# Column-tiled lone score tiles, the sync queue in the scheduler, and newly searched limits in an attention kernel

## The chip, the cores and the metric

The kernel runs on one core of one Trainium2 chip. The metric is device time in microseconds (us). A ratio is the mean time of one kernel's fast runs over that of the kernel before in the same rounds, so it is not quite the ratio of the medians that stand beside it.

In the profile lines, PE is the matrix engine TensorE, PEld its weight load, DVE is VectorE, ACT is ScalarE, POOL is GpSimd, and SP is the sync engine that issues most transfers ("SPq").

## The reference, cut to what matters

Two attention layers read the same input, and a gate mixes their results. Layer A is full softmax attention with 32 heads of size 16 over 2048 positions. Layer B is a local one with a window of 8.

```python
def _A_ref(x, wqkv, wo):
    ...                                   # q, k, v = x @ wqkv, H = 32 heads, Dh = 16
    scores = jnp.einsum("bhqd,bhkd->bhqk", q, k) * Dh ** -0.5
    o = jnp.einsum("bhqk,bhkd->bhqd", softmax(scores), v)
    return o... @ wo
def _B_ref(x, wqkv, wo): ...              # keys at distance 0, 2, .., 14 only
g = sigmoid((x * gate_w).sum(-1, keepdims=True))
return g * _A_ref(x, A_wqkv, A_wo) + (1 - g) * _B_ref(x, B_wqkv, B_wo)
```

## The kernel before

The scores of A are cut into 2048 tiles of 128 keys by 512 queries. They are worked through in 32 blocks of 64 tiles (one query chunk and one set of four heads per block). Each tile's exponential is computed either by ScalarE (`pt`), two or three tiles at a time, or by VectorE (`yb`), which approximates it with integer arithmetic: one pass per tile and two more passes over batches of up to four tiles. Only six of the sixteen key tiles (`KD`) may go to VectorE. A score matmul reads 32 rows (four heads' 16-wide keys sit in four row groups), so it is row-tiled; nearly every other matmul of the kernel is column-tiled (128 rows, 32 columns, four at a time).

The instruction order is not written by hand. While the kernel is built, a list scheduler in Python plays a timeline with its own constants (a matmul counts 0.216 us, a switch of tiling mode 0.11 us) and emits each instruction when its turn comes. Its decisions depend on limits such as these; eleven of them are given per stretch, 64 stretches in all, as strings of digits.

```python
MM = 0.216
SWITCH = 0.11
D_LAST = 58
...
def d_wanted(now, flex=True):            # may a tile go to VectorE now?
    if p >= N - 8 or p % 64 >= D_LAST or not any(k in KD for r in rem[p // 64] for k in r):
        return False                     # p: number of score tiles handed out so far
    ...
    ready = [s for s in self.steps if s.rel <= p and s.eng in ("PE", "DVE") and ready_time(s) <= now + 1.5]
    ...
    load = max(0.0, t["DVE"] - now) + sum(s.cost for s in ready if s.eng == "DVE")
    return load < tune("backlog" if flex else "backlog_s")
...
# TensorE has nothing better to do: a "lone" tile for VectorE, by itself
elif fits(MM + SWITCH - tune("alone")) and d_wanted(now) and self.kq_ok(rem, geo, p, 4, now):
    emit_qk([d_take([])], [], now)
...
# transfers: s.n is the number of issues, T_SP = 0.55 us each
sp = now0 + s.n * T_SP
```

The sixteen small copies of the gate are issued inside a VectorE step (`gate_t`), so this account of the queue doesn't see them.

## Time and profile before

| | before |
|---|---|
| time, median (of three runs) | 733.99 us (732.43 to 734.55) |
| span in the profile | 731.1 us |
| busy ACT, DVE, PE | 705.8, 673.8, 694.4 us |
| score tiles exponentiated by DVE, by ACT | 526, 1522 |

From the page of the kernel before: busy times, then the span in 40 slices, each digit the busy share in tenths.

```profile
span 731.1 us, 20619 instructions
...
PE 694.4 (95%) x8304; PEld 225.8 (31%) x8304; DVE 673.8 (92%) x1149; ACT 705.8 (97%) x704; POOL 206.5 (28%) x218
...
DVE  6897999998999999999999999999999998998884
ACT  6998999999999999999999999999999999999994
```

ScalarE is the limit: it is full from the third slice to the last but one, save for the fourth, where the stall shown below lies. VectorE has some room all along, so the way to be faster is to move tiles from ScalarE to VectorE. The groups of instructions by shape (count | busy us, mean ns of one | idle time before them and what ended it) show what a tile costs:

```profile
L1855 ACT ACTIVATE pt<-fps 128x1024 bf16<-128x1024 f32 x546 | 531.0, 1089 | 8.4 <-PE fps L1801 6.4 <-PE fps L1605 1.2
L1533 DVE TENSOR_SCALAR yb<-fps 128x512 int16<-128x512 f32 x526 | 340.4, 683 | 21.5 <-PE fps L1801 20.0
...
L1855 ACT ACTIVATE pt<-fps 128x1536 bf16<-128x1536 f32 x143 | 217.4, 1520 | 2.9 <-PE fps L1801 2.4
```

ACT handles 546 x 2 + 143 x 3 tiles in these, and one more by itself, in 700 us: 0.46 us a tile. VectorE waited 20 us in all for a score matmul (line 1801) to give it a tile.

The timeline of TensorE around a lone tile (start, duration, instruction, count). Durations of matmuls include their latency; what counts is the distance of the starts.

```profile
401.69 0.39 PE L1605 MATMUL fps<-pt,vaug 128*32 128x512 bf16 x1
401.69 0.40 PE L1605 MATMUL fps<-yb,vaug 128*32 128x512 f16 x2
401.70 0.39 PE L1605 MATMUL fps<-pt,vaug 128*32 128x512 bf16 x1
402.02 0.38 PE L1801 MATMUL fps<-qm,kT 32*128 32x512 bf16 x1
402.33 0.40 PE L1517 MATMUL fps<-wz 128*32 128x512 bf16 x4
```

The row-tiled tile starts 0.32 us after the four column-tiled matmuls and holds the next ones off for 0.31 us; where four column-tiled matmuls follow four others, the starts are about 0.22 us apart (405.30 and 405.52 us in the same trace).

One stall stands out. The waits of TensorE, the sync queue's issues between 30 and 64 us, and the table of windows (busy us of each engine in each stretch, then granted clock, DMA share, GB/s):

```profile
PE fps L881 <- DMA ww<-in_B_wqkv_dram: 2.7, 1, 2.7
```

```profile
36.80 10.78 SPq L1121 DMA_DIRECT2D gA<-gs  x16
47.69 10.64 SPq L948 DMA_DIRECT2D qm<-qs  x16
58.37 0.58 SPq L876 DMA_DIRECT2D ww<-in_B_wqkv_dram  x1
```

```profile
54.00:58.00 4.00, 4.00 (x59) 1.42 (x59) 3.97 (x8) 4.00 (x5) 1.30 (x2) 1.00 0.11 27
58.00:62.00 4.00, 1.34 (x22) 0.43 (x21) 1.06 (x3) 1.59 (x3) 4.00 (x5) 1.00 0.18 41
62.00:66.00 4.00, 4.00 (x39) 0.76 (x30) 2.70 (x4) 3.37 (x3) 0.77 (x1) 0.57 0.00 0
```

The columns after the stretch's length are PE, PEld, DVE, ACT, POOL. A weight load is issued only at 58.4 us, behind 32 small copies that took the queue 21 us, and all of TensorE, VectorE and ScalarE stand still for it.

### The profile page before, as it was taken

What the parts mean: (1) busy time and instruction counts of PE and PEld (TensorE: products, weight loads), DVE (VectorE), ACT (ScalarE), POOL (GpSimd) and SP (SyncE); (2) the same over time, 40 slices, a digit from 0 to 9 for tenths busy, and PEclk for the clock granted to TensorE, in tenths of its full rate; (3) what the DMA queues carried; (4) which work ended last, traced back from release to release, by engine and by line L of the source; (5) the groups of instructions that cost most, each with busy time, mean ns of one, the idle gap of its engine ahead of it and who ended that gap; (6) DMA issues with size and microseconds to landing.
All of it is one profiled execution on the core that took longest, in us unless ns stands there. A gap on an engine that the chain in (4) does not pass through costs nothing.

```text
span 731.1 us, 20619 instructions
## 1 busy us (share of the span) xinstructions
PE 694.4 (95%) x8304; PEld 225.8 (31%) x8304; DVE 673.8 (92%) x1149; ACT 705.8 (97%) x704; POOL 206.5 (28%) x218
## 2 busy tenths in 40 slices
PE   9998999999998999999999999999999999999996
PEld 4432333333332323332222323323222322222342
DVE  6897999998999999999999999999999998998884
ACT  6998999999999999999999999999999999999994
POOL 2134000000003322222000456555545635256100
PEclk9999999999999999999999999999999999999999
DMA  6000201000000100001033446474464552284000
GB/s 167 3 13 22 58 2 39 1 30 4 8 8 1 24 1 6 4 1 39 8 71 101 120 112 163 127 174 125 127 162 114 155 147 79 75 181 116 9 31 28
DMA packets 63720, 48.54 MB, mean 66 GB/s; under 512 B 21760, under 2 KB 63232, under 8 KB 63488
## 3 DMA queue, kind: packets, MB, share of 16 engines
q1 hardware_dynamic: 62912, 45.70, 24.8%
q8 instruction: 67, 1.10, 0.6%
q0 software_dynamic: 288, 1.05, 0.4%
q14 instruction: 37, 0.30, 0.2%
q10 hardware_dynamic: 416, 0.39, 0.2%
HBM read 39.85 MB, written 5.26 MB: 62 GB/s over the span
## 4 chain that ended last, share of the span: by engine, by line
ACT 39%; PE 30%; DVE 13%; issue 11%; SPq 2%; DMA 2%; POOL 1%; ACTq 0%; DVEq 0%; POOLq 0%
ACT pt L1855 38%; PE fps L1801 11%; PE fps L1605 10%; PE fps L881 7%; DVE yb L1533 6%; DVE yb L1539 3%; SPq L948 2%; DMA vw<-v_dram 1%; PE fps L1350 1%; DVE prod L1201 1%; POOL erb L1332 1%; DVE t L1637 1%; PE fps L1215 1%; PE fps L954 0%; ACT er L1220 0%
## 5 line engine op out<-in xcount | busy, mean ns | idle before, releaser
L1855 ACT ACTIVATE pt<-fps 128x1024 bf16<-128x1024 f32 (+1 forms) x690 | 700.0, 1178 | 11.4 <-PE fps L1801 8.8
L1533 DVE TENSOR_SCALAR yb<-fps 128x512 int16<-128x512 f32 x526 | 340.4, 683 | 21.5 <-PE fps L1801 20.0
L1801 PE MATMUL fps<-qm,kT 32*128 32x512 bf16 x2048 | 308.8, 383 | 21.5 <-ACT pt L1855 16.0
L1605 PE MATMUL fps<-pt,vaug 128*32 128x512 bf16 (+1 forms) x1618 | 247.9, 374 | 0.1
L1801 PEld LDWEIGHTS <-kT 32*128 32x128 bf16 x2048 | 91.0, 91 | 283.3 <-issue 276.1
L1539 DVE TENSOR_SCALAR yb<-yb 128x2048 int16<-128x2048 int16 (+3 forms) x280 | 177.7, 665 | 0.8
L1605 PE MATMUL fps<-yb,vaugw 128*32 128x512 f16 (+1 forms) x1116 | 163.8, 372 | 2.1 <-DVE yb L1539 2.0
L881 PE MATMUL fps<-xT,ww 128*32 128x512 bf16 (+2 forms) x1296 | 99.4, 381 | 4.4 <-DMA ww<-in_B_wqkv_dram 2.7
L1332 POOL TENSOR_TENSOR er<-er,vw 128x512 bf16<-128x512 bf16 x64 | 72.4, 1156 | 108.3 <-DMA erb<-er_dram 63.7
L1605 PE MATMUL fps<-yb,vaug 128*32 128x512 f16 (+1 forms) x558 | 99.3, 372 | 0.1
L1605 PEld LDWEIGHTS <-vaug 128*32 128x32 bf16 x2176 | 68.2, 94 | 95.2 <-issue 87.8
L1332 POOL TENSOR_TENSOR erb<-erb,vw 128x512 bf16<-128x512 bf16 x64 | 73.2, 1164 | 72.8 <-DVE yb L1539 28.8
L1201 POOL TENSOR_TENSOR prod<-bq,bk 128x512 bf16<-128x512 bf16 x32 | 34.0, 1075 | 128.1 <-DVE yb L1539 78.9
L1605 PEld LDWEIGHTS <-vaugw 128*32 128x32 bf16 x1116 | 44.2, 95 | 41.6 <-issue 35.9
L881 PEld LDWEIGHTS <-ww 128*32 128x32 bf16 x1296 | 26.4, 95 | 36.3 <-issue 25.1
L1201 DVE TENSOR_TENSOR prod<-bq,bk 128x2048 bf16<-128x2048 bf16 x24 | 28.7, 1222 | 0.4 <-PE fps L1215 0.4
L1628 DVE STREAM_TRANSPOSE t<-fps 128x512 f32<-128x512 f32 x32 | 22.7, 709 | 4.5 <-PE fps L1605 4.5
L1124 POOL DMA_DIRECT2D wAv<-in_A_wo_dram x1 | 0.8, 757 | 85.4 <-PE fps L1801 85.4
L881 PE MATMUL fps<-woB,oB 128*32 128x512 bf16 x256 | 20.5, 383 | 0.0
L881 PE MATMUL fps<-wAv,oT 128*32 128x512 bf16 x256 | 19.5, 384 | 0.1
L881 PE MATMUL fps<-wAv,xT 128*32 128x128 bf16 (+1 forms) x512 | 18.3, 274 | 0.0
L909 DVE CAST vaug<-fps 128x384 bf16<-128x384 f32 (+1 forms) x24 | 12.2, 509 | 4.8 <-PE fps L881 4.4
(112 smaller groups left out, 277.7 us busy)
## 6 DMA issues: line engine op xcount, KB each, us to landing
vw<-v_dram SPq DMA_DIRECT2D x128, 128.0 KB, 3.2
er<-er_dram SPq DMA_DIRECT2D x128, 64.0 KB, 3.0
erb<-er_dram SPq DMA_DIRECT2D x128, 64.0 KB, 2.9
v_dram<-vs SPq DMA_DIRECT2D x16, 128.0 KB, 3.0
out_dram<-ob SPq DMA_DIRECT2D x15, 128.0 KB, 1.7
qm<-qs SPq DMA_DIRECT2D x112, 16.0 KB, 1.8
x_in<-in_A_x_dram SPq DMA_DIRECT2D x3, 512.0 KB, 6.1
ww<-in_B_wqkv_dram SPq DMA_DIRECT2D x12, 128.0 KB, 2.7
```

What stands on the lines that cost most here:

```text
L881: self.nc.tensor.matmul(out=out_ps[32 * c:32 * c + 32, 0:n], lhsT=lhsT_of(c), rhs=rhs, start=start, stop=stop, tile_position=(0, 32 * c))
L909: self.nc.vector.tensor_copy(out=self.vaug4[:, st0:st0 + nst, h0:h1, 0:DH], in_=self.misc[:, 0:nst * n].rearrange("p (t h e) -> p t h e", ...
L948: self.nc.sync.dma_start(out=self.qm[i % NQM][r][k:k + 16, :], in_=self.qs[i % 2][k:k + 16, :])
L1201: return e.tensor_tensor(out=pr[m % 2][:, a:b], in0=bq[ct][:, a:b], in1=bk[ct][:, o + a:o + b], op=ALU.mult)
L1215: nc.tensor.matmul(out=self.misc[32 * sc:32 * sc + 32, :], lhsT=self.Eh[:, ct, :], rhs=pr[m % 2][:, sc * 512:(sc + 1) * 512], start=(ct == ...
L1332: return nc.gpsimd.tensor_tensor(out=st_["erb"][m % 4][:, g, :], in0=st_["erb"][m % 4][:, g, :], in1=st_["vw"][m % 2][:, g, :], op=ALU.mult)
L1533: return nc.vector.tensor_scalar(out=self.yb[bt["buf"]][:, 0, i * 512:(i + 1) * 512], in0=bank[:], scalar1=A, scalar2=1024.0 * (15.0 + PW_ ...
L1539: return nc.vector.tensor_scalar(out=y[:, k, 0:n], in0=y[:, 0, 0:n], scalar1=float(round(1024.0 * (PW_S[k] - PW_S[0]))), scalar2=None, op0 ...
L1605: nc.tensor.matmul(out=out, lhsT=v, rhs=r, start=start, stop=stop, tile_position=(0, 32 * j))
L1628: nc.vector.transpose(out=self.t1[:, par].rearrange("p a b -> p (a b)"), in_=self.flex[acc[b]])
L1801: nc.tensor.matmul(out=dst, lhsT=self.kT[ct % 2][32 * j:32 * j + 32, kt * 128:(kt + 1) * 128], rhs=self.qm[(4 * ct + qc) % NQM][par][32 * ...
L1855: nc.scalar.activation(out=self.pt[pi[0]][pi[1]][:, 0:n * 512], in_=self.aslot[si][:, 0:n, :].rearrange("p a b -> p (a b)"), func=ACT.Exp, ...
```

## The change

Its intent, in three parts. (1) Lone tiles need no change of tiling mode: for key tile 9, each head's keys are copied into a tile of 128 rows that is zero elsewhere, so that a score matmul can use all 128 rows and be split into four column tiles. (2) The scheduler's account of the sync queue includes the gate copies, and some issue counts are raised. (3) All limits and several constants are set anew; a beam search chose the digits of the 64 stretches.

```diff
+KZ = (9,)
+TUNE = dict(R0=74, R1w=42, R1g=20, ..., ahead=0.142, ..., dlast=62, ..., prelB=59, prodrel=-12)
 LEVELS = dict(                      # every level list replaced
-    backlog=(1.5, 2.2, 3.0, 3.8, 5.0),
+    backlog=(0.758, 1.231, 1.61, 1.894, 2.273, 2.841, 3.788),
 ...
 STRETCH = dict(                     # every string replaced
-    grab="2222222222222222222222222222222222122221222222222222222222212222",
+    grab="0000040200000000000000000000000000000200040020000000000000000030",
 ...
+        self.kz = c([P, 4, len(KZ), P], BF16, name="kz")           # zeroed once
-        self.wz = c([P, 512], BF16, name="wz")                      # makes room for kz
+        self.wz = c([P, P], BF16, name="wz")
+    def k_spread(self, ct, kt):
+        for j in range(4):
+            r = slice(32 * j, 32 * j + 32)
+            self.nc.sync.dma_start(out=self.kz[r, j, KZ.index(kt), :], in_=self.kT[ct % 2][r, P * kt:P * kt + P])
...
-                wl = self.dma(... self.load_w("B", kind, ct), 6.0, rel=R0 + 16 * n - 44)
+                wl = self.dma(... self.load_w("B", kind, ct), 6.0, rel=R0 + 16 * n - U["prelB"])
-        self.gate_done = Step("DVE", 1.5, gate_t, deps=[ch[-1]], due=50, cls=1, lat=4.0)
+        self.gate_done = Step("DVE", 1.5, gate_t, deps=[ch[-1]], due=50, cls=1, lat=14.0)
+        self.gate_done.dn = 19                                       # issues in the sync queue
...
-        R0 = 64                                                      # branch B's projections start from this score tile on
+        R0 = U["R0"]                                                 # 74
...
-            if p >= N - 8 or p % 64 >= D_LAST or ...
+            if p >= N - 8 or p % 64 >= TUNE["dlast"] or ...
-            ready = [... ready_time(s) <= now + 1.5]
+            ready = [... ready_time(s) <= now + TUNE["ahead"]]
...
+        def emit_alone(d, now):
+            for c in range(4):
+                nc.tensor.matmul(out=dst[32 * c:32 * c + 32, :], lhsT=self.kz[:, j, KZ.index(kt), 32 * c:32 * c + 32],
+                                 rhs=self.qm[(4 * ct + qc) % NQM][par][:], start=True, stop=True, tile_position=(0, 32 * c))
+            t["PE"] = now + k * MM + (SWITCH if mode == "r" else 0.0)
+            mode = "c"
...
-                    elif fits(MM + SWITCH - tune("alone")) and d_wanted(now) and self.kq_ok(...):
+                    elif spread(now) and fits(MM - tune("alone")) and d_wanted(now):
+                        emit_alone(d_take([], True), now)
+                    elif not spread(now) and fits(MM + SWITCH - tune("alone")) and d_wanted(now) and self.kq_ok(...):
```

More of the change, by code (lines that the diff above doesn't have):

```diff
@@ L53 @@
 YB_ITEMS = 4
+TUNE = dict(R0=74, R1w=42, R1g=20, R2g=31, R3g=46, R3w=50, dueB=61, dueL=84, v2rel=79, v2step=21, v2due=91, krel=230, krel2=192, ahead=0.142, dueV=30, dueS=115, dueO=678, dlast=62, qrel=28, prelB=59, prodrel=-12)
 LEVELS = dict(
-    backlog=(1.5, 2.2, 3.0, 3.8, 5.0),
-    backlog_s=(0.5, 1.0, 1.5, 2.2, 3.0),
-    part_us=(1.5, 2.2, 3.0, 4.0, 6.0),
-    misc_slack=(-20, -8, 0, 8, 20),
-    urgent=(0, 4, 8, 16, 32),
-    fit=(-0.2, 0.0, 0.2, 0.4, 0.6),
-    port=(0.3, 0.6, 0.9, 1.2, 2.0),
@@ L63 @@
-    alone=(-9.0, -0.2, 0.0, 0.2, 9.0),
-    grab=(0, 1, 4, 2, 1),
-    lend=(0, 1, 3, 2, 7),
-    order=((-1, 1, 0, 2, 3), (-1, 0, 2, 1, 3), (-1, 0, 1, 2, 3), (-1, 0, 1, 2, 1), (1, 0, 1, 2, 3)),
+    backlog=(0.758, 1.231, 1.61, 1.894, 2.273, 2.841, 3.788),
+    backlog_s=(0.888, 1.442, 1.886, 2.219, 2.663, 3.329, 4.438),
+    part_us=(0.6, 0.975, 1.275, 1.5, 1.8, 2.25, 3.0),
+    misc_slack=(-32, -18, -12, -8, -4, 2, 16),
+    urgent=(-25, -11, -5, -1, 3, 9, 23),
+    fit=(0.0, 0.2, 0.3, 0.4, 0.5, 0.6, 0.8),
@@ L67 @@
+    port=(0.338, 0.549, 0.718, 0.845, 1.014, 1.268, 1.69),
+    alone=(-8.973, -0.273, -0.123, 0.027, 0.177, 0.327, 9.027),
+    grab=(1, 0, 2, 3, 4),
+    lend=(1, 0, 2, 3, 4, 5, 6, 7),
+    order=((-1, 0, 1, 2, 1), (-1, 1, 0, 2, 3), (-1, 0, 2, 1, 3), (-1, 0, 1, 2, 3), (1, 0, 1, 2, 3), (0, 0, 1, 2, 3), (1, 0, 2, 1, 3), (2, 0, 1, 2, 3)),
 )
 STRETCH = dict(
-    backlog="1111111111131111111111111111111111111111111111111111211111111111",
-    backlog_s="3333333333333333333333333333333333333333333333333333133333333233",
@@ L71 @@
-    part_us="0000010000040000000000000000000000000000000000000000000000000000",
-    misc_slack="1111111111111111111111111111111111111111111111111111111111111111",
-    urgent="0000000000000000000000000000000000000000000000000000000000000000",
-    fit="3333333333333333333333333333333333333333333333333333333333333332",
-    port="2222222222232222222222222222222222222222222222222222432222222222",
-    alone="2222221222122222222222222222222222322222222222222222122212222222",
-    grab="2222222222222222222222222222222222122221222222222222222222212222",
@@ L78 @@
-    lend="1111111111111111111111111111111111011111111111111111111111111111",
-    order="4144444444444444444444444444444444444144444444444444444444444444",
+    backlog="3333333333333333333633333333433363534333333336633333333333334336",
+    backlog_s="3333333333333333333333330333333323353333333333333433333332333033",
+    part_us="3353333536333603130313333336033313303333443333303332433333333333",
+    misc_slack="3333331333333333333333333333235533333333033233333333333333333333",
+    urgent="3333333433333333333333333333364313333336233333333333335333333333",
@@ L80 @@
+    fit="3533331313633333333333333303333332333303133533333333133303333333",
+    port="3333333333333333333333333333433334333333334433333333543333633333",
+    alone="3331332033330333333333333333335323333333333333333333433333333333",
+    grab="0000040200000000000000000000000000000200040020000000000000000030",
+    lend="0000000300060000000001000000500000000000000000002000600000000000",
+    order="1000000700000000000005410000407010000000400000000000100200000000",
 )
 SLOT_D = 3
-D_LAST = 58
 X_LAND = (0, 1.7, 3.7, 5.2)
@@ L702 @@
     __slots__ = ("eng", "cost", "fn", "deps", "due", "cls", "rel", "acq", "free", "lat", "end", "on_done", "hold",
-                 "chain", "port", "n")
+                 "chain", "port", "n", "dn")
     def __init__(self, eng, cost, fn, deps=(), due=0.0, cls=2, rel=-1, acq=False, free=False, lat=0.1,
@@ L711, in __init__ @@
         self.n = 1
+        self.dn = 0.0
 T_ACT = lambda n: n / 1200.0 + 0.063
@@ L833, in setup @@
         nc.vector.memset(warm[:], 0.0)
-        nc.vector.memset(self.wz[:, P:512], 0.0)
         nc.scalar.activation(out=warm[:], in_=warm[:], func=ACT.Exp)
@@ L851, in setup @@
         nc.gpsimd.memset(self.vaug[:, NKT * H * VS:NKT * H * VS + 32], 0.0)
+        nc.gpsimd.memset(self.kz[:], 0.0)
         for w, v, v4 in zip(PW_W[1:], self.vw[1:], self.vw4[1:]):
@@ L1040, in jobs @@
                 wl = self.dma(lambda ct=ct: (self.load_w("A", "k", ct), self.load_w("A", "q", ct)), 6.0,
-                              rel=base - 290)
+                              rel=base - 290, n=2)
             for sc in range(4):
@@ L1053, in jobs @@
                     if ct:
-                        rel = base - 230 + 16 * sc
+                        rel = base - TUNE["krel"] + 16 * sc
                         if ct >= 2:
-                            rel = base - 64 * 3 + 16 * sc
+                            rel = base - TUNE["krel2"] + 16 * sc
                     else:
@@ L1066, in jobs @@
                         ("DVE", T_D1(512), lambda ct=ct, sc=sc: self.q_stage(ct, sc))],
-                        due=qd - 8, rel=base + 128 * sc - 128 * (NQM - 1) + 4, deps=dep)
+                        due=qd - 8, rel=base + 128 * sc - 128 * (NQM - 1) + TUNE["qrel"], deps=dep)
                     qd = [ch[-1]]
@@ L1075, in jobs @@
                     qdone[(ct, sc)] = self.dma(lambda ct=ct, sc=sc: self.q_split(ct, sc), T_LAND, deps=qd,
-                                               n=16 if (ct, sc) == (3, 3) else 8)
+                                               n=20 if (ct, sc) == (3, 3) else 10)
         for st in range(0, NKT, 2):
@@ L1088, in jobs @@
                                  for k in range(1, NP_) if st in KD],
-                            due=512 - 100 + 4 * st, rel=80 + 20 * st)
+                            due=512 - TUNE["v2due"] + 4 * st, rel=TUNE["v2rel"] + TUNE["v2step"] * st)
             for ct in range(1, 4):
@@ L1092, in jobs @@
         self.kdone, self.qdone, self.vdone = kdone, qdone, vdone
+        self.kzdone = {(ct, kt): self.dma(lambda ct=ct, kt=kt: self.k_spread(ct, kt), T_LAND, deps=[kdone[(ct, kt // 4)]],
+                                          rel=512 * ct if ct else 4, due=512 * ct + 16 * (kt // 4), n=4)
+                       for ct in range(4) for kt in KZ}
         self.xs = xs
@@ L1143, in b1_open @@
                 pr[i] = BP["1"].tile([P, S], BF16, name=f"prod{i}")
-        R0 = 64
+        U = TUNE
+        R0 = U["R0"]
         o1 = self.dma(b1_open, 0.5, rel=R0, deps=self.x_done)
@@ L1171, in jobs_b @@
             for kind in ("q", "k"):
-                wl = self.dma(lambda ct=ct, kind=kind: self.load_w("B", kind, ct), 6.0, rel=R0 + 16 * n - 44)
+                wl = self.dma(lambda ct=ct, kind=kind: self.load_w("B", kind, ct), 6.0, rel=R0 + 16 * n - U["prelB"])
                 for sc in range(4):
@@ L1182, in jobs_b @@
                             self.proj_mm(self.w_tiles[("B", kind, ct)], (2, 3), sc)),
-                        ("DVE", T_D1(512), ev)], due=R0 + 16 * n + 60, rel=R0 + 16 * n, deps=[wl, o1])
+                        ("DVE", T_D1(512), ev)], due=R0 + 16 * n + U["dueB"], rel=R0 + 16 * n, deps=[wl, o1])
                     evs[(ct, kind, sc)] = ch[-1]
                     n += 1
-        R1 = R0 + 16 * n + 20
+        R1 = R0 + 16 * n + U["R1g"]
         allp = list(evs.values())
         exps = []
-        R1w = 44
+        R1w = U["R1w"]
         lgs = []
@@ L1206, in jobs_b @@
                     else:
-                        s = Step("DVE", T_D2(S), prod, deps=deps, rel=R1 + R1w * w + 8 * ct, due=R1 + R1w * w + 60,
+                        s = Step("DVE", T_D2(S), prod, deps=deps, rel=R1 + R1w * w + 8 * ct + U["prodrel"], due=R1 + R1w * w + 60,
                                  cls=3)
@@ L1223, in jobs_b @@
             ch = self.chain([("PE", MM, lambda ct=ct, w=w: lg(ct, 4 * w + ct)) for ct in range(4)] +
-                            [("ACT", T_ACT(512), ex)], due=R1 + R1w * w + 70, deps=pd[:2])
+                            [("ACT", T_ACT(512), ex)], due=R1 + R1w * w + U["dueL"], deps=pd[:2])
             for ct in range(4):
@@ L1231, in jobs_b @@
             exps.append(ch[-1])
-        R2 = R1 + R1w * WIN + 30
+        R2 = R1 + R1w * WIN + U["R2g"]
         st_ = {}
@@ L1281, in jobs_b @@
         wls = self.dma(lambda: [self.load_w("B", "v", ct) for ct in range(4)], 6.0, deps=exps, n=4)
-        R3 = R2 + 40
-        R3w = 50
+        R3 = R2 + U["R3g"]
+        R3w = U["R3w"]
         prods_of = {}
@@ L1310, in jobs_b @@
                     ("PE", 2 * MM, lambda ct=ct, sc=sc: self.proj_mm(self.w_tiles[("B", "v", ct)], (2, 3), sc)),
-                    ("DVE", T_D1(512), vev)], due=R3 + R3w * i - 30, rel=R3 + R3w * i - 40,
+                    ("DVE", T_D1(512), vev)], due=R3 + R3w * i - U["dueV"], rel=R3 + R3w * i - 40,
                     deps=[wls] + ([prods_of[("vd", i - 2)]] if i >= 2 else []))
@@ L1355, in oev @@
                     nc.vector.tensor_copy(out=st_["oB"][ct][:, sc * 512:(sc + 1) * 512], in_=self.misc[:])
-                ch = self.chain([("PE", 2 * MM, sm), ("DVE", T_D1(512), oev)], due=R3 + R3w * i + 60, deps=pd)
+                ch = self.chain([("PE", 2 * MM, sm), ("DVE", T_D1(512), oev)], due=R3 + R3w * i + U["dueS"], deps=pd)
                 prods_of[("sum", 2 * i)] = prods_of[("sum", 2 * i + 1)] = ch[0]
@@ L1494, in run @@
         tail_norm = Step("X", 0, None)
+        xdone = Step("X", 0, None)
+        xdone.end = 0.0
         table = {k: [v[int(c)] for c in STRETCH[k]] for k, v in LEVELS.items()}
         def tune(k):
-            return table[k][min(p, N - 1) // 32]
+            return table[k][min(p, N - 1) * len(table[k]) // N]
         def did_work(now, n):
@@ L1516, in filler @@
             for j in js:
-                nc.tensor.matmul(out=self.flex[acc[cur]][32 * j:32 * j + 32, :], lhsT=self.wz[:, 0:32], rhs=self.wz[:],
+                nc.tensor.matmul(out=self.flex[acc[cur]][32 * j:32 * j + 32, :], lhsT=self.wz[:, 0:32],
+                                 rhs=self.wz[:].unsqueeze(1).to_broadcast([P, 4, P]),
                                  start=False, stop=False, tile_position=(0, 32 * j))
@@ L1678, in norm_steps @@
                 for st in range(4 * qc, 4 * qc + (2 if last else 4)):
-                    self.chain(self.outproj_specs(st), due=64 * b + (100 if last else 500), rel=-1,
+                    self.chain(self.outproj_specs(st), due=64 * b + (100 if last else TUNE["dueO"]), rel=-1,
                                deps=[s3] + [self.oB_done[(qc, c)] for c in range(4)])
@@ L1689, in take_step @@
         def take_step(s, eng, now):
-            nonlocal port_last
+            nonlocal port_last, sp
             if s.acq:
@@ L1701, in take_step @@
             s.end = now + s.cost + s.lat
+            if s.dn:
+                sp = max(sp, now + s.cost) + s.dn * T_SP
             if s.free:
@@ L1724, in d_wanted @@
         def d_wanted(now, flex=True):
-            if p >= N - 8 or p % 64 >= D_LAST or not any(k in KD for r in rem[p // 64] for k in r):
+            if p >= N - 8 or p % 64 >= TUNE["dlast"] or not any(k in KD for r in rem[p // 64] for k in r):
                 return False
@@ L1731, in d_wanted @@
                 return False
-            ready = [s for s in self.steps if s.rel <= p and s.eng in ("PE", "DVE") and ready_time(s) <= now + 1.5]
+            ready = [s for s in self.steps if s.rel <= p and s.eng in ("PE", "DVE") and ready_time(s) <= now + TUNE["ahead"]]
             if flex and any(s.acq and s.due <= p + tune("misc_slack") for s in ready):
@@ L1736, in d_wanted, with spread, draw @@
             return load < tune("backlog" if flex else "backlog_s")
-        def draw(used, dve=False):
+        def spread(now):
+            b = p // 64
+            if b >= NB - 2:
+                return False
+            ct = geo(b)[0]
+            return any(k in KZ for r in rem[b] for k in r) and all(
+                self.kzdone[(ct, k)].end is not None and self.kzdone[(ct, k)].end <= now for k in KZ) \
+                and self.qdone.get((ct, geo(b)[1]), xdone).end <= now
+        def draw(used, dve=False, lone=False):
             nonlocal p
             b = p // 64
-            js = [j for j in range(4) if (any(k in KD for k in rem[b][j]) if dve else rem[b][j])]
+            js = [j for j in range(4) if (any(k in (KZ if lone else KD) for k in rem[b][j]) if dve else rem[b][j])]
             js = [j for j in js if j not in used] or js
@@ L1751, in draw @@
             p += 1
-            kt = next((k for k in rem[b][j] if (k in KD) == dve), rem[b][j][0])
+            own = [k for k in rem[b][j] if (k in KD) == dve] or rem[b][j]
+            kt = next((k for k in own if not dve or (k in KZ) == lone), own[0])
             rem[b][j].remove(kt)
@@ L1779, in d_add, with d_take @@
             return it, bank[:], d0
-        def d_take(used):
-            it = draw(used, True)
+        def d_take(used, lone=False):
+            it = draw(used, True, lone)
             fi = min(range(4), key=lambda i: fx_free[i])
@@ L1794, in slot_done @@
                 slot_free[si] = slot_end[si]
+        def emit_alone(d, now):
+            nonlocal mode
+            (b, kt, j), dst, d0 = d
+            ct, qc, par = geo(b)
+            for c in range(4):
+                nc.tensor.matmul(out=dst[32 * c:32 * c + 32, :], lhsT=self.kz[:, j, KZ.index(kt), 32 * c:32 * c + 32],
+                                 rhs=self.qm[(4 * ct + qc) % NQM][par][:], start=True, stop=True, tile_position=(0, 32 * c))
+            k = slow(now)
+            did_work(now, 512)
+            t["PE"] = now + k * MM + (SWITCH if mode == "r" else 0.0)
+            mode = "c"
+            d0.end = t["PE"] + 0.25
+            if batch is not None and p < N and p - 64 * batch["blk"] >= TUNE["dlast"]:
+                close_batch()
         def emit_qk(dv, ac, now):
@@ L1810, in emit_qk @@
                 d[2].end = t["PE"] + 0.25
-            if batch is not None and p < N and p - 64 * batch["blk"] >= D_LAST:
+            if batch is not None and p < N and p - 64 * batch["blk"] >= TUNE["dlast"]:
                 close_batch()
@@ L1977, in run @@
                         did = True
-                    elif fits(MM + SWITCH - tune("alone")) and d_wanted(now) and self.kq_ok(rem, geo, p, 4, now):
+                    elif spread(now) and fits(MM - tune("alone")) and d_wanted(now):
+                        emit_alone(d_take([], True), now)
+                        did = True
+                    elif not spread(now) and fits(MM + SWITCH - tune("alone")) and d_wanted(now) and self.kq_ok(rem, geo, p, 4, now):
                         emit_qk([d_take([])], [], now)
```

## The prediction

> **What bounds the kernel.** ScalarE (ACT). The page gives ACT 705.8 of 731.1 us (97%), PE 95%, VectorE (DVE) 92%. In the table of windows ACT is busy 36.1 to 36.6 of 36.55 us nearly everywhere, except in the first two of 20 slices (28.6, 31.7) and the last (27.3). ACT's idle time: about 5 us before 10 us, 7.6 us from 10 to 75, 3.3 us from 75 to 720, 3.3 us in the tail. ACT exponentiates 1522 of the 2048 score tiles (groups by form: 143 activations of three tiles, 546 of two; 700 us, 0.46 us per tile). DVE takes 526, at 0.65 us (line 1533) plus 0.34 us (line 1539), about 0.98 us each. DVE idles 57 us, 33 us of it between 75 and 720; 20 us of the waits end on a score matmul.
>
> **One stall.** At 58 to 62 us ACT is busy 1.6 of 4 us and PE 1.3: projection matmuls wait 2.7 us for a branch-B weight load in the sync queue; in the next 4 us the granted clock is 0.57.
>
> **What the change does.**
> 1. Lone tiles. Today one is a 32-row matmul between column-tiled ones. The Trainium skill (TensorEngine Tiling, Key Properties) says that a change of tiling mode drains the TensorE. The trace agrees: from a row-tiled burst of one to three matmuls to the next burst takes 0.31 to 0.32 us, entering it 0.31 us, while four column-tiled matmuls issue in about 0.22 us. With zero-spread keys the lone tile stays in column mode: 0.22 us instead of about 0.42. But the timeline has only 23 bursts of one row matmul: at most 5 us of PE. Only key tile 9 qualifies (120 tiles), so more lone tiles become possible, each 0.22 us of a full PE. Added: 16 small transfers. Nearly neutral alone.
> 2. DMA queue in the scheduler: gate copies count as 19 issues, B weights are asked for earlier; the stall should shrink: about 3 us of ACT.
> 3. Searched limits. Grabs per slot fall to one, the look-ahead of the load test from 1.5 to 0.14 us, the block end moves from 58 to 62: DVE gets tiles more readily and evenly. I expect 10 to 20 more tiles on DVE (536 to 546), each worth 0.46 us of ACT: 5 to 9 us. DVE rises to 94 or 95%.
>
> **Sum.** 734 - 4 (stall, early idle) - 7 (tiles moved) - 2 (other idle, wider activations) = 721 us, an estimate from these durations. All of it lies on the critical path, as ACT does. I doubt more: at 715 us ACT and DVE would both be almost without idle.
>
> Predicted 721 us, range 711 to 731; faster by over 2% 0.38, within 2% 0.60, slower 0.02.
>
> **What would show it.** Step 1: column-tiled score matmuls reading kz, 4 per tile, 100 to 480 of them, and few bursts of one row matmul. Step 2: no ACT gap over 1 us between 40 and 75 us. Step 3: over 526 exp instructions on DVE, fewer tiles on ACT, DVE idle below 45 us, ACT idle about 14 us.
>
> **What would make it wrong.** The tile count on DVE not rising (then 726 to 730); the search having fitted the scheduler's own model, so that engines meet waits it doesn't see; more sharing of the third PSUM bank (more two-wide activations, up to 6 us of ACT overhead); PE, at 95%, becoming the limit through the extra column matmuls. Conversely, if DVE reaches 97%, about 715.

## The result, and the profile after

The kernel after took 714.58 us (714.31 to 714.89), the kernel before 734.27 us in the same rounds. The ratio of the fast runs is 0.9737, with a 95% interval of 0.972 to 0.9754: faster by 2.6%.

The page of the kernel after, and its groups by shape:

```profile
span 712.6 us, 21088 instructions
...
PE 684.4 (96%) x8522; PEld 222.2 (31%) x8522; DVE 685.5 (96%) x1184; ACT 694.4 (97%) x702; POOL 206.0 (29%) x219
...
DVE  6999999999999999999999999999999999999994
ACT  6999999999999999999999999999999999999994
```

```profile
L1900 ACT ACTIVATE pt<-fps 128x1024 bf16<-128x1024 f32 x564 | 546.1, 1104 | 2.8 <-PE fps L1846 2.2 <-ACT pt L1900 0.2
L1551 DVE TENSOR_SCALAR yb<-fps 128x512 int16<-128x512 f32 x548 | 355.7, 678 | 5.8 <-PE fps L1846 3.0 <-PE fps L1831 0.9
...
L1900 ACT ACTIVATE pt<-fps 128x1536 bf16<-128x1536 f32 x124 | 192.2, 1550 | 1.2 <-PE fps L1846 1.0
...
L1831 PE MATMUL fps<-qm,kz 128*32 128x512 bf16 x312 | 33.4, 384 | 0.4 <-DVE yb L1551 0.3
```

VectorE took 548 tiles, 22 more. The 18.5 us that the span lost are 11.4 us of ScalarE's busy time (705.8 to 694.4) and 7.1 us of its idle time (25.3 to 18.2); the two always add up to the span. VectorE's idle time before its exponentials fell from 21.5 to 5.8 us, and its whole idle time from 57.3 to 27.1 us. Lone tiles on zero-spread keys number 312 / 4 = 78.

The chain of work that ended last, by engine, first before and then after:

```profile
ACT 39%; PE 30%; DVE 13%; issue 11%; SPq 2%; DMA 2%; POOL 1%; ACTq 0%; DVEq 0%; POOLq 0%
```

```profile
PE 48%; ACT 30%; DVE 9%; issue 8%; SPq 3%; DMA 2%; ACTq 0%; DVEq 0%
```

After the change ScalarE, TensorE and VectorE are busy 97, 96 and 96% of the span, and the chain passes more through TensorE than through ScalarE. So ScalarE no longer looks like the only limit.

The stall at 58 us is gone. The table of windows after, and the queue's issues:

```profile
58.00:62.00 4.00, 4.00 (x50) 1.18 (x47) 4.00 (x8) 4.00 (x6) 2.71 (x4) 1.00 0.37 84
62.00:66.00 4.00, 4.00 (x56) 1.15 (x52) 3.93 (x9) 4.00 (x5) 1.65 (x2) 1.00 0.01 4
```

```profile
32.52 11.05 SPq L1134 DMA_DIRECT2D gA<-gs  x16
43.68 10.73 SPq L952 DMA_DIRECT2D qm<-qs  x16
54.46 2.97 SPq L880 DMA_DIRECT2D ww<-in_B_wqkv_dram  x3
```

The 32 copies take the queue as long as before, but end 4 us earlier, and TensorE doesn't need the weights before they are there: the scheduler also releases branch B's projections ten score tiles later (`R0`, 64 to 74).

A third reading, worked out from the two traces: each idle gap of VectorE between 10 and 690 us is put at the position, in its block of 64, of the score tile that TensorE was to start next when the gap began. Idle us of VectorE by eighth of the block, all blocks together:

| kernel | 1st | 2nd | 3rd | 4th | 5th | 6th | 7th | 8th | sum |
|---|---|---|---|---|---|---|---|---|---|
| before | 14.6 | 8.6 | 2.1 | 2.9 | 1.3 | 2.3 | 2.2 | 5.0 | 39.0 |
| after | 1.2 | 1.7 | 0.9 | 2.0 | 0.2 | 2.4 | 0.8 | 2.2 | 11.4 |

Before, 23 of 39 us lay in the first quarter of the blocks. (Put by the middle or the end of the gap, some of these us change places between the eighths. The last eighth and the first quarter together, the turn of the block, have 26 to 28 us by each of these rules.) This is the shape that `D_LAST = 58` would make: the last six tiles of a block may not go to VectorE, so it runs dry at the turn of the block. The count of VectorE exponentials that start at positions 60 to 63 or 0 to 3 rose from 21 + 5 to 37 + 20 by the same rule. An experiment has to show that the limit does it.

### The profile page after: what moved, and what is told of

It is laid out like the page before. It is cut to its first block, busy times and chain, and to the rows that moved or that the text cites. A ratio compares the mean times of both kernels' runs of the same rounds, so it can differ in the third digit from the quotient of the medians.

```text
span 712.6 us, 21088 instructions
## 1 busy us (share of the span) xinstructions
PE 684.4 (96%) x8522; PEld 222.2 (31%) x8522; DVE 685.5 (96%) x1184; ACT 694.4 (97%) x702; POOL 206.0 (29%) x219
## 4 chain that ended last, share of the span: by engine, by line
PE 48%; ACT 30%; DVE 9%; issue 8%; SPq 3%; DMA 2%; ACTq 0%; DVEq 0%
ACT pt L1900 29%; PE fps L1846 17%; PE fps L1623 15%; PE fps L885 13%; DVE yb L1551 4%; DVE yb L1557 2%; SPq L1315 1%; DMA er<-er_dram 1%; PE fps L1831 1%; PE fps L1365 1%; ACT er L1235 1%; SPq L952 1%; DMA x_in<-in_A_x_dram 1%; DVE prod L1216 0%; SPq L1341 0%
## 5 line engine op out<-in xcount | busy, mean ns | idle before, releaser
L1900 ACT ACTIVATE pt<-fps 128x1024 bf16<-128x1024 f32 (+1 forms) x688 | 688.9, 1184 | 4.0 <-PE fps L1846 3.2
L1551 DVE TENSOR_SCALAR yb<-fps 128x512 int16<-128x512 f32 x548 | 355.7, 678 | 5.8 <-PE fps L1846 3.0
L1846 PE MATMUL fps<-qm,kT 32*128 32x512 bf16 x1970 | 287.2, 383 | 17.6 <-ACT pt L1900 15.1
L1623 PE MATMUL fps<-pt,vaug 128*32 128x512 bf16 (+1 forms) x1596 | 238.1, 373 | 0.2 <-DVE kT L927 0.2
L1557 DVE TENSOR_SCALAR yb<-yb 128x2048 int16<-128x2048 int16 (+3 forms) x294 | 183.3, 647 | 0.6
L1623 PE MATMUL fps<-yb,vaugw 128*32 128x512 f16 (+1 forms) x1160 | 174.0, 372 | 0.5 <-DVE yb L1557 0.2
L1846 PEld LDWEIGHTS <-kT 32*128 32x128 bf16 x1970 | 84.6, 91 | 278.3 <-issue 272.7
L1623 PE MATMUL fps<-yb,vaug 128*32 128x512 f16 (+1 forms) x580 | 106.0, 372 | 0.1
L1831 PE MATMUL fps<-qm,kz 128*32 128x512 bf16 x312 | 33.4, 384 | 0.4 <-DVE yb L1551 0.3
L885 PE MATMUL fps<-woB,oB 128*32 128x512 bf16 x256 | 19.7, 382 | 0.0
L1167 POOL TENSOR_TENSOR er<-xT 128x512 bf16<-128x512 bf16 x8 | 8.1, 1039 | 37.3 <-DVE yb L1557 37.3
```

Source lines behind the costliest of these rows:

```text
L885: self.nc.tensor.matmul(out=out_ps[32 * c:32 * c + 32, 0:n], lhsT=lhsT_of(c), rhs=rhs, start=start, stop=stop, tile_position=(0, 32 * c))
L1167: return nc.gpsimd.tensor_tensor(out=sq(sc, kc), in0=x, in1=x, op=ALU.mult)
L1551: return nc.vector.tensor_scalar(out=self.yb[bt["buf"]][:, 0, i * 512:(i + 1) * 512], in0=bank[:], scalar1=A, scalar2=1024.0 * (15.0 + PW_ ...
L1557: return nc.vector.tensor_scalar(out=y[:, k, 0:n], in0=y[:, 0, 0:n], scalar1=float(round(1024.0 * (PW_S[k] - PW_S[0]))), scalar2=None, op0 ...
L1623: nc.tensor.matmul(out=out, lhsT=v, rhs=r, start=start, stop=stop, tile_position=(0, 32 * j))
L1831: nc.tensor.matmul(out=dst[32 * c:32 * c + 32, :], lhsT=self.kz[:, j, KZ.index(kt), 32 * c:32 * c + 32], rhs=self.qm[(4 * ct + qc) % NQM][ ...
```

## The experiments

Twelve kernels ran; all results were correct. The theory after reading the traces: the gain is (a) about 4 us from the stall and (b) the rest from VectorE being fed at the turn of the blocks and by more freely placed lone tiles; the mode switch itself is worth nothing. The rivals: the saved mode switches; or the search, which may have found one lucky order.

### The mode switch by itself

The same order of instructions on every engine as in the kernel after; only the emission of a lone tile differs:

```diff
-            for c in range(4):
-                nc.tensor.matmul(out=dst[32 * c:32 * c + 32, :], lhsT=self.kz[:, j, ...], rhs=self.qm[...][par][:], ..., tile_position=(0, 32 * c))
+            nc.tensor.matmul(out=dst, lhsT=self.kT[ct % 2][32 * j:32 * j + 32, kt * 128:(kt + 1) * 128],
+                             rhs=self.qm[...][par][32 * j:32 * j + 32, :], ..., tile_position=(32 * j, 0))
```

> The kernel after, with every instruction in the same order on every engine, except that each of the 78 lone score tiles is again one 32-row matmul instead of four column matmuls on zero-spread keys. Theory A (the mode switch is paid on TensorE and TensorE is close to the limit): each lone tile costs about 0.2 us more of TensorE, 15 us in all, and since TensorE idles only about 28 us a part of it reaches ScalarE: 717 to 725 us, with ScalarE idle up. Rival B (column mode matters only as a thing that lets the scheduler place more tiles, TensorE has slack): within 2 us of 714.6.

Measured: 715.09 us (714.67 to 715.69), ratio 0.974 against 0.9737: the same. My expectation of 717 to 725 us failed. TensorE was busy 683.2 us, even 1.2 us less than with column tiles. The timelines show why. First the kernel after, then the experiment, at the same place in the order:

```profile
37.76 0.61 PE L885 MATMUL fps<-xT,ww 128*32 128x512 bf16 x8
38.20 0.39 PE L1831 MATMUL fps<-qm,kz 128*32 128x512 bf16 x4
38.52 0.39 PE L1846 MATMUL fps<-qm,kT 32*128 32x512 bf16 x2
38.84 0.62 PE L885 MATMUL fps<-xT,ww 128*32 128x512 bf16 x8
```

```profile
37.83 0.61 PE L885 MATMUL fps<-xT,ww 128*32 128x512 bf16 x8
38.37 0.38 PE L1830 MATMUL fps<-qm,kT 32*128 32x512 bf16 x1
38.38 0.39 PE L1846 MATMUL fps<-qm,kT 32*128 32x512 bf16 x2
38.70 0.61 PE L885 MATMUL fps<-xT,ww 128*32 128x512 bf16 x8
```

Here a burst of row-tiled matmuls follows the lone tile anyway. The row-tiled lone tile starts 0.01 us before it, in another row group, and costs nothing of its own: the whole piece takes 0.87 us, against 1.08 us with four column tiles. Of some 70 groups of lone tiles in the kernel after, only about ten lie between column-tiled matmuls on both sides, where column mode saves about 0.2 us each (0.43 us from the burst before to the burst after, against 0.63); the others touch a row-tiled burst, where it costs between nothing and about 0.2 us each (starts compared in both traces). The two nearly cancel. The zero-spread keys as such bring nothing in this order.

### How much lies in the one order that was found

```diff
-MM = 0.216
+MM = 0.2159
```

This is the scheduler's own constant. The hardware's work is the same, but the order comes out differently from the first decision that falls the other way, and the digits of the 64 stretches no longer fit it. The value was chosen as one for which the scheduler builds a schedule for all the variants below; for several others it runs into a dead end with one of them. By the scheduler's own timeline it is neither the best nor the worst of some two dozen close values.

> The kernel after with nothing changed but the scheduler's own constant for a matmul, 0.2159 for 0.216 us. The hardware does the same work, but the instruction order comes out differently, so the searched limits no longer fit it. Theory A (a good part of the speed lies in this one order that the search found): 725 to 731 us, with 526 tiles on VectorE instead of 548. Rival B (the speed lies in the mechanisms, the order is robust): 713 to 717 us.

> The kernel before with the same constant at 0.2159. Theory A (the order of before was a searched one too, so it loses as much): 743 to 750 us, with 505 tiles on VectorE; then the step from before to after is about as large between two unsearched orders, 15 to 20 us, and the search is not what the gain comes from. Rival B (before was not much searched): 732 to 737 us.

> The kernel after at a third value of the scheduler's matmul constant, 0.21618 us: one more order that nobody searched, to see how far such orders lie apart (e2_after_mm took 728.8 us). Theory A (orders scatter by a few us around a typical value far above the searched one): 726 to 736 us, with 515 to 525 tiles on VectorE. Rival B (e2 was an unlucky one, the typical order is near the searched one): 714 to 722 us.

Measured: 728.76 us (728.26 to 729.71) for the kernel after at 0.2159, with 526 tiles on VectorE; 731.85 us (731.7 to 732.3) at 0.21618, with 517 tiles; 748.73 us (745.38 to 749.21) for the kernel before at 0.2159, with 505 tiles. So a constant changed by less than 0.1% costs 14 to 17 us in the kernel after and 14 us in the kernel before. Both searches found orders far better than the ones their settings give untuned. The step between untuned orders, 748.7 to 728.8 or 731.9, is 17 to 20 us: about as large as that between the two tuned ones. So a search as such is not what tells the kernels apart; how much of the step is the search's constants shows below. It also follows that "undo one part" is only clean between orders that nobody searched, and that such orders scatter: the two of the kernel after lie 3 us and 9 tiles apart. Two orders only bound the scatter from below, and of the kernel before one untuned order alone was run.

### The stall

The kernel before in its own order, with one branch-B weight tile loaded at the start into a tile of its own:

```diff
+        nc.sync.dma_start(out=self.wb0[:], in_=self.wsrc["B"][:, :, 0:P])       # e4: queries; e4b: keys, D:D + P
...
+        if (br, kind, ct) == ("B", "q", 0):                                      # e4b: ("B", "k", 0)
+            self.w_tiles[(br, kind, ct)] = self.wb0
+            return
```

> The kernel before in its own order, with one transfer moved: the first branch-B weight tile, for which TensorE stood still at 58 us behind 32 copies in the sync queue, is loaded into a tile of its own at the start. (The zero tile for filler matmuls shrinks as in the kernel after, to make room.) Theory A (that stall is on the critical path): the ScalarE gap of 2.4 us at 62 us is gone, as are the cold clock and the stall of TensorE, and the time falls by 3 to 4.5 us, to 729.5 to 731. Rival B (the gap is given back later): within 1 us of before.

Measured: 734.16 us (731.49 to 735.0), ratio 0.9985: nothing. It was the wrong tile. TensorE's wait and the queue's issue of a weight at the same place were still there:

```profile
PE fps L885 <- DMA ww<-in_B_wqkv_dram: 3.0, 1, 3.0
```

```profile
48.16 10.64 SPq L952 DMA_DIRECT2D qm<-qs  x16
58.85 0.58 SPq L880 DMA_DIRECT2D ww<-in_B_wqkv_dram  x1
```

> As e4_early_weight, but with the right tile: the trace of that run shows that the matmuls at 58 us wait for the second branch-B weight tile (keys), whose load is issued at 58.4 us behind 32 copies. It is now loaded at the start; the order of everything else is that of the kernel before. Theory A (the stall is on the critical path): no wait of TensorE for a weight near 58 us, the ScalarE gap near 62 us is gone, 729.5 to 731.5 us. Rival B (given back later): within 1 us of before.

Measured: 730.44 us (729.97 to 730.8), ratio 0.9947 (0.9912 to 0.9983), so about 4 us. Its table of windows:

```profile
58.00:62.00 4.00, 3.98 (x53) 1.30 (x53) 3.45 (x7) 4.00 (x5) 4.00 (x5) 1.00 0.05 12
```

ScalarE and TensorE are full where they stood still. ScalarE's idle time between 10 and 75 us fell from 7.6 us in the trace of the kernel before to 4.1 us. The span fell by 2.5 us, with a period of 3.4 us at half clock at 476 us that the other trace doesn't have. So the stall was on the critical path, and most of it is not given back; the interval, 1 to 6.5 us, doesn't tell its size closely.

Which part of the change removes it? The kernel after at 0.2159, with the scheduler as blind to the queue as before, but the weights still asked for early:

```diff
-        self.gate_done = Step("DVE", 1.5, gate_t, deps=[ch[-1]], due=50, cls=1, lat=14.0)
-        self.gate_done.dn = 19
+        self.gate_done = Step("DVE", 1.5, gate_t, deps=[ch[-1]], due=50, cls=1, lat=4.0)
...                                   # and the issue counts 10 -> 8, 20 -> 16, 2 -> 1
```

> The kernel after at the constant 0.2159 (e2_after_mm, 728.8 us) with the scheduler blind to the sync queue as before: gate copies counted as no issues, query copies as 8 and not 10, weight pairs as one. Theory A (the scheduler now keeps its orders free of the stall that cost before some 4 us): TensorE waits over 1 us for a weight or a query copy between 40 and 75 us again, 733 to 740 us. Rival B (the earlier request for the weights alone removes the stall, the accounting adds nothing but another order): no such wait, and 725 to 738 us, which the scatter of orders would explain.

Measured: 739.17 us (737.94 to 739.7), 10 us above e2_after_mm, with 514 tiles on VectorE. But TensorE waits for no weight and no query copy in the trace. So the early part of Rival B holds: the stall stays away without the new accounting. The time is 1.2 us outside Rival B's range all the same, and inside Theory A's, whose mechanism failed. A thing that the expectation didn't know: in this order TensorE falls to half clock at 306.9 us for 10.2 us and at 685.8 us for 6.8 us, which happens nowhere in e2_after_mm before its tail. But which engine takes a tile is fixed when the kernel is built, so the clock can act only through ScalarE's idle time. Of the 9.9 us between the two spans 6.2 us are ScalarE's busy time (12 more tiles) and 3.7 us its idle time; the clock's part is at most about the latter. What the accounting is worth stays open. It is not needed to keep the stall away. What does keep it away was not isolated: the weights' earlier request, the later start of the projections (`R0`), or copies that end earlier. In the kernel after the load still goes out right behind the copies, at 54.5 us.

### The limit at the end of a block

```diff
-D_LAST = 58
+D_LAST = 62
```

in the kernel before at 0.2159, and the reverse in the kernel after at 0.2159:

> The kernel before at the constant 0.2159 (e3_before_mm, 748.7 us) with one limit changed: VectorE may take score tiles up to position 62 of a block's 64, not 58. Theory A (VectorE starves at the block's turn; this limit is a main part of the gain): VectorE idle falls most in the first quarter of the blocks, 515 to 520 tiles on VectorE, 736 to 741 us. Rival B (an unsearched order differs by some us anyway and the limit does nothing): 745 to 750 us.

> The kernel after at the constant 0.2159 (e2_after_mm, 728.8 us) with that limit back at 58. Theory A: 735 to 740 us, about 511 tiles on VectorE, its idle time again in the first quarter of the blocks. Rival B: 726 to 731 us.

Measured: 735.88 us (735.8 to 736.24) for the kernel before with 62, which is 12.9 us less than e3_before_mm, with 518 tiles on VectorE in place of 505. And 735.63 us (734.98 to 735.78) for the kernel after with 58, which is 6.9 us more than e2_after_mm, with 511 tiles in place of 526. VectorE's idle time by eighth of the block, as in the table above:

| kernel, at 0.2159 | 1st | 2nd | 3rd | 4th | 5th | 6th | 7th | 8th | sum |
|---|---|---|---|---|---|---|---|---|---|
| before, 58 (e3) | 16.0 | 11.2 | 3.1 | 4.6 | 6.1 | 2.5 | 3.2 | 18.3 | 65.0 |
| before, 62 (e5) | 7.9 | 8.5 | 4.2 | 3.9 | 5.2 | 4.4 | 4.3 | 6.7 | 45.1 |
| after, 62 (e2) | 7.5 | 6.5 | 6.2 | 2.8 | 0.5 | 2.2 | 4.5 | 4.9 | 35.0 |
| after, 58 (e6) | 16.5 | 9.7 | 4.7 | 3.0 | 3.9 | 6.5 | 3.7 | 4.7 | 52.6 |

In both directions the idle time at the turn of the block (last eighth and first quarter) moves with the limit: 45.5 to 23.1 us, and 18.9 to 30.9 us. The other untuned orders of the kernel after with 62 bear it out: e8, e7 and e9 have 19.0, 21.7 and 20.3 us there, so the 30.9 us of e6 are not scatter. That the limit starves VectorE at the turn is shown. What it is worth is less certain. The pairs differ by 7 and 13 us, but against e8 (731.85 us, also with 62) e6 is only 3.8 us slower, about as far as e8 is from e2. The clock is not the cause between e2 and e6: of the 5.3 us between their spans ScalarE's busy time, which the build fixes, makes up 6.2 us, and its idle time fell by 0.9 us. Between e3 and e5 busy time makes up 6.7 of 13.2 us; the other 6.5 us are idle time, in which the clock can have a part: apart from the stall and the tail, e3 has two periods of 6.8 us at half clock and e5 one; e2 has none and e6 one of 3.4 us.

### The lone tiles' price

The kernel after at 0.2159 without zero-spread keys: no copies, and `spread` always false, so that a lone tile is row-tiled, and the scheduler adds the switch of 0.11 us to it.

> The kernel after at the constant 0.2159 (e2_after_mm, 728.8 us) without the zero-spread keys: no copies, lone tiles row-tiled and priced so by the scheduler. e1_row_lone showed that the emission itself is worth nothing. Theory A (the column price still lets the scheduler place lone tiles that it would not place otherwise): 733 to 740 us with 510 to 515 tiles on VectorE. Rival B (nothing is lost): 726 to 731 us.

Measured: 734.72 us (734.66 to 735.46), 6 us above e2_after_mm, 512 tiles on VectorE in place of 526. VectorE waited 32.0 us before its exponentials, 29.9 of them for a score matmul, against 22.9 and 19.0 us in e2_after_mm. Two periods at half clock, 10.2 us together, are not the cause: ScalarE's busy time rose by 6.4 us and its idle time fell by 1.4 us. But against e8_after_mm_other, an untuned order with the keys, the loss is only 2.9 us and 5 tiles, no more than e2 and e8 lie apart. So this run only suggests that the keys, which don't pay on TensorE (e1_row_lone), pay through the scheduler, by letting it place a lone tile that it believes to be cheap more often or at better times. That is argued, not shown: a search at the dear price was not run.

### Is the column mode needed for that? And is the order special?

Two attempts at a version that beats both. The first drops the zero-spread keys, emits lone tiles row-tiled from any of the six key tiles of VectorE, but keeps the cheap price:

```diff
-        self.kzdone = {(ct, kt): self.dma(lambda ct=ct, kt=kt: self.k_spread(ct, kt), ...)}
+        self.kzdone = {}
...
         def spread(now):
+            return True                          # for all but the last two blocks
-                        emit_alone(d_take([], True), now)
+                        emit_alone(d_take([]), now)
...                                              # emit_alone as in e1_row_lone; new digits for the 64 stretches
```

The second is the kernel after with new digits alone. Both sets of digits come from a beam search of mine over the scheduler's timeline.

> An attempt at a better kernel: the kernel after without zero-spread keys and their copies; a lone tile is a single row-tiled matmul, may come from any of the six key tiles that VectorE takes and not only tile 9, and the scheduler prices it as if no mode switch were paid (e1_row_lone says that this is about true). The limits of the 64 stretches are searched anew for it by a beam of mine over the scheduler's own timeline. Theory A (the zero-spread keys only serve to justify the price; placement and search make the speed): 713 to 718 us with about 544 tiles on VectorE. Rival B (without the keys, row-tiled lone tiles in all places cost TensorE time the scheduler does not see): 720 us or more.

> The kernel after, its zero-spread keys included, with limits from that same beam of mine in place of its own: another searched order. Theory A (any order that is searched as hard gets about there, the particular one does not matter): 714 to 719 us with about 545 tiles on VectorE. Rival B (the searched order of the kernel after is special on the chip): 722 us or more.

Measured: 718.57 us (718.32 to 718.94), ratio 0.9796 (0.9779 to 0.9813, so whether it is 2% faster is unclear), with 544 tiles on VectorE, and 716.13 us (715.88 to 716.37), ratio 0.9761, with 546 tiles. Neither beats the kernel after. f2_col_searched says that its order isn't special: another one, searched as hard, comes within 1.6 us. f1_row_searched is half a microsecond outside Theory A's range and still below Rival B's; without a single zero-spread key it has 14.9 of the gain of 19.7 us. So column mode is not necessary for most of the gain; it may be worth a few us at most with a tuned order, and this pair can't say whether the rest is column mode or the luck of a search.

## Why the prediction was right

The time was inside the range (714.58 us against 711 to 731), but 6.4 us below its centre, and the odds leaned to "within 2%", which did not come true.

- **The limit (right).** ScalarE was the limit before (97%), and taking tiles and idle time from it gave the gain, as foreseen. After the change it is still the busiest (97%), but TensorE is about as tight: it has 48% of the chain that ended last, ScalarE 30%. The risk that I named, that extra column matmuls would make TensorE the limit, did not cost time: without them, e1_row_lone took 715.09 us.
- **Step 1, lone tiles (right about TensorE, incomplete about the scheduler).** "Nearly neutral alone" is what e1_row_lone measured, 715.09 against 714.58 us. But the reason was other than given: I priced a lone tile at 0.42 us before and 0.22 us after, and missed that a row-tiled one beside a row-tiled burst runs along with it. So the right result is partly luck. There are 312 column-tiled score matmuls, inside 100 to 480; bursts of one row-tiled matmul fell from 23 to 6. The Trainium skill (TensorEngine Tiling, Key Properties) says that a change of mode drains the TensorE; the trace agrees (0.31 to 0.32 us between bursts against 0.22), so the drain is paid per change, not per tile. What the cheaper price is worth for the placement (6 or 3 us in e7_after_mm_no_lone, by the order that it is compared with, so not clear of the scatter) was only hinted at, "more lone tiles become possible".
- **Step 2, the queue (right in size, one part of the cause not shown).** "About 3 us of ACT": e4b_early_k_weight gives 4.3 us between the medians (1 to 6.5 us). No gap of ScalarE over 1 us was left between 40 and 75 us. The accounting, which I named first, isn't needed to remove the stall (e9_after_mm_queue_blind). The weights' earlier request, the later start of the projections, which I overlooked, and another order of the copies remain; none was tested alone.
- **Step 3, the limits (right mechanism, term too small).** "10 to 20 more tiles on DVE" was 22, and "5 to 9 us" was about 10 us (22 x 0.46) of the 11.4 us by which ScalarE's busy time fell. I named the three changes but sized none of them. The block's end is the only one of the three that was tested: 7 to 13 us between pairs of untuned orders, 4 us against a third. The grabs and the look-ahead were not tested. The block's end could have been read beforehand: 23 of VectorE's 39 us of idle time lay in the first quarter of the blocks.
- **The other idle time (too small).** I allowed 4 us for the stall and the early idle time and 2 us for the rest; ScalarE's idle time fell by 7.1 us. VectorE idles 27.1 us (foreseen: below 45). ScalarE's 18.2 us are 12.6 us without the time after its last activation, which my "about 14 us" left out. My view that at 715 us both engines would be almost without idle time was about right: by their gaps, between 75 and 660 us VectorE idles 7.6 us and ScalarE 1.1 us. What failed was the doubt that this could be reached.
- **The sum.** Foreseen -13 us; measured -19.7 us between the medians. The missing part is mostly the tiles (about 4 us of ScalarE's busy time) and about 1 us of idle time; the rest lies between the span and the measured time.
- **What I didn't think of.** Both kernels are searched orders, 14 to 17 us better than what their settings give for a constant that is barely different.

## What to carry to other kernels

Before pricing a change of a scheduler's limits, plot the idle time of the engine that should get more work against the scheduler's own period (here the block): a limit such as "not in the last six tiles" shows as a bump, and one number may be worth more than a new data layout. Where one engine is the limit and the build fixes its work, split a difference into that engine's busy and idle time: a change of clock can only be in the idle part. When an instruction order comes out of a search, a part of the change can't be undone in it and compared; either keep the order and change one instruction's form (as in e1_row_lone and e4b_early_k_weight), or compare orders that nobody searched, and more than one of each: here two of them lay 3 us apart, as much as some of the effects sought. A switch of tiling mode is paid once per burst: an extra matmul of the minority mode is cheap if it is put beside others of its kind.

## What the Trainium skill lacked or had wrong

- **TensorEngine Tiling (Key Properties, Performance Considerations).** It says that a mode change drains the TensorE, and gives no number. Here a burst of one to three row-tiled 32x512 matmuls between column-tiled ones takes 0.31 to 0.32 us to the next burst, against 0.22 us for four matmuls without a change, so about 0.1 us per change.
- **TensorE: Matmul & The Clock Gate (HAM oscillation — how this bites in real kernels).** It gives the rule as "no PE-idle gaps >~3.4µs". In the kernel before, a single gap of 2.66 us (to 60.81 us) is followed by half clock for 3.4 us. In e9_after_mm_queue_blind, where no matmul begins after an idle gap of even 1 us, the clock records show half clock for 10.2 us at 306.9 us and 6.8 us at 685.8 us. The table of windows around the first of them has TensorE busy for 3.38 of 4 us just before:

```profile
302.00:306.00 4.00, 3.38 (x31) 1.10 (x29) 3.97 (x8) 4.00 (x5) 1.04 (x1) 1.00 0.01 2
306.00:310.00 4.00, 3.69 (x29) 0.92 (x27) 2.21 (x5) 4.00 (x4) 1.04 (x1) 0.61 0.00 0
```

  So short gaps added up, with few matmuls at a time, seem to be enough. The page's next section (A second HAM failure mode: psum-queue depth-cycling) does tell of short idle times that throttle, but gives no length for them; what exactly is counted stays open. That the records know only full and half speed, as the page says, holds in all these traces of one core.
- **DMA: Bandwidth & Descriptors (Issuing engines are not separate DMA queues).** It calls the sequencer's issue time "usually small relative to the DMA itself" and gives none for small copies on the sync engine; elsewhere the page has a figure for GpSimd's path, and a count of cycles per transfer for "previous generations" beside its trn3 figures. Here each of 32 small copies took the queue about 0.67 us (10.78 us for 16 and 10.64 us for 16), enough to hold up a weight load behind them and cost some 4 us of kernel time (1 to 6.5).
- No page says how far a run time depends on the instruction order alone: here three orders of one kernel, whose scheduler's constants differ by less than 0.1%, took 714.6, 728.8 and 731.9 us.
